# A recurrent attention layer and two gated matrix layers on one core: 64-row transposes on two banks, weight narrowing spread out, and another order of the large units

## The chip, the cores and the metric

The kernel runs on one core of a Trainium2 chip. The metric is the device time of one execution in microseconds (us); lower is better. The kernel before took 459.11 us, the median of three runs (457.83 to 459.53).

The engines are called by the names of the profile: PE is the matrix engine (PEld its weight loads), DVE the vector engine, ACT the scalar engine, POOL the GpSimd engine, and SP the engine that here issues DMAs and empty instructions that only wait. Each engine has its own queue and takes it in order.

## The reference

An mLSTM recurrence (2 batches, 8 heads, 768 steps, head dimension 40) gives 1536 token rows of 320 values, and two gated layers follow, each with three weight matrices of 320x1536, 320x1536 and 1536x320:

```python
def _moe_ref(x, w_gate, w_val, w_out):
    gate = 1.0 / (1.0 + np.exp(-(x @ w_gate)))
    val = x @ w_val
    return (gate * val @ w_out).astype(np.float32)

def _moe2_ref(x, w_a, w_b, w_out):
    a = x @ w_a
    b = x @ w_b
    return (a * b @ w_out).astype(np.float32)
```

The weights of the layers arrive as 64-bit floats and are narrowed on the core. Every product is made of three in the PE's short format: high by high, high by low and low by high, where "low" is what the rounding to "high" left over.

## The kernel before, in words

**Order.** The whole program is one list of task names, the string `PLAN` (lines 67 to 130). The loop at line 890 walks it and calls each task's function (`tasks`, lines 742 to 873), and every engine gets its instructions in that order. A suffix names the engine where a task may run on several: `:V` is DVE, `:G` is POOL, `:A` is ACT. The list also fixes which buffer a task gets: `pick` (line 879) gives it the one whose readers stand earliest in the list. There are two buffers each of `mm1`, `e`, `acc` and `y`, all PSUM banks (line 724).

**Stages.** Up to about 133.6 us the recurrence (24 half steps) is interleaved with 24 small units of the first layer. Then come 60 large units, units 24 to 83. A segment is four large units that share four token tiles of 128 rows and four accumulators: segments 8 to 13 finish the first layer, 14 to 22 make the second.

**A large unit u** takes one chunk (128 of the 1536 hidden columns) and four token tiles (512 rows). On PE it is four tasks, each made of pairs of matmuls on the two 64-row halves of the array (`side_by_side`, line 542): `ma` (8 pairs) and `mb` (7 pairs) make both products into two banks, one `mm1` and one `e`; `mm` and `mn` (6 pairs each) multiply the gated result into the four accumulators. `mb` and `mn` start with a handshake: an empty instruction on SP waits for the last matmuls of `ma` or `mm`, and the first pair of `mb` or `mn` waits for it (lines 544 to 553). It stands in SP's queue between the DMA issues. Between `mb` and `mm` lie `ga_` (ACT, L598: copies one product, with the sigmoid in the first layer), `gm` (DVE, L603: times the other), `gh_` (ACT, L609: the high part) and `gl_` (DVE, L614: the low part). `ma` of unit u+2 needs the banks of unit u, so it waits for `ga_` and `gm` of u.

**A segment's end.** Four tasks `ev<segment>.<tile>` empty the accumulators (L704 adds into `x2tok`; L702 or, on ACT, L700 where it is the first segment of a layer). The first `mm` of the next segment needs the same four banks: its first three pairs need one `acc` and one `y` bank, its last three the other two.

**A weight chunk c** is loaded by `w` (960 KB, SP, L209) and narrowed: `na` (ACT, two instructions, L216 and L217), `nb`, `ns`, `nc` (DVE, L223, L228, L234), `nd` (L240), then split: `s1` (ACT, L250 to L252), `s2` (L256), `s3` (L260, L261). `na` needs the landed data and the one `cva` buffer that `nd` of the chunk before gives back; `w` needs a `wst` buffer that `s2` and `s3` of chunk c-2 give back.

**Between the layers** each of the 12 token tiles is transposed: `yt` (PE, three transposes, L485), `yh` (ACT, L494, the high part) and `yl` (DVE, L498, the low part) write the second layer's input.

Of the kernel before, what the change touches and what calls it, by code (L numbers as in the profile page):

```python
# [96 lines left out]
ma31 ga_30 gm30 mm29 gh_30 gl_30 mb31 s110 mn29 ma32 ga_31 gm31 mm30 gh_31 gl_31 s210:G s310:V mb32 na11 mn30
ma33 ga_32 gm32 mm31 gh_32 gl_32 nb11 ns11 mb33 nc11 nd11:V mn31 w12 ma34 ga_33 ev9.5 ev9.7 ev9.4 ev9.6 gm33
mm32 gh_33 gl_33 mb34 s111 mn32 ma35 ga_34 gm34 mm33 gh_34 gl_34 s211:G s311:V mb35 na12 mn33 ma36 ga_35 gm35
mm34 gh_35 gl_35 nb12 ns12 mb36 nc12 nd12:V mn34 w13 ma37 ga_36 gm36 mm35 gh_36 gl_36 mb37 s112 mn35 ma38  # L100
ga_37 ev10.11 ev10.9 ev10.8 ev10.10 gm37 mm36 gh_37 gl_37 s212:G s312:V mb38 na13 mn36 ma39 ga_38 gm38 mm37
gh_38 gl_38 nb13 ns13 mb39 nc13 nd13:V mn37 w14 ma40 ga_39 gm39 mm38 gh_39 gl_39 mb40 s113 mn38 ma41 ga_40
gm40 mm39 gh_40 gl_40 s213:G s313:V mb41 na14 mn39 ma42 ga_41 ev11.0 ev11.1 ev11.2 ev11.3 gm41 mm40 gh_41
gl_41 nb14 ns14 mb42 nc14 nd14:V mn40 w15 ma43 ga_42 gm42 mm41 gh_42 gl_42 mb43 s114 mn41 ma44 ga_43 gm43 yt0
mm42 yh0 yl0 gh_43 gl_43 s214:G s314:V mb44 na15 mn42 ma45 ga_44 gm44 yt1 mm43 yh1 yl1 gh_44 gl_44 nb15 ns15
mb45 nc15 nd15:V mn43 w16 ma46 ga_45 ev12.4 ev12.6 ev12.5 ev12.7 gm45 yt2 mm44 yh2 yl2 gh_45 gl_45 mb46 s115
mn44 ma47 ga_46 gm46 yt3 mm45 yh3 yl3 gh_46 gl_46 s215:G s315:V mb47 na16 mn45 ma48 ga_47 gm47 yt4 mm46 yh4
yl4 gh_47 gl_47 nb16 ns16 mb48 nc16 nd16:V mn46 w17 ma49 ga_48 gm48 yt6 mm47 yh6 yl6 gh_48 gl_48 mb49 s116
mn47 ma50 ga_49 ev13.10 ev13.8 ev13.11 ev13.9 gm49 yt5 mm48 yh5 yl5 gh_49 gl_49 s216:G s316:V mb50 na17 mn48
ma51 ga_50 gm50 yt7 mm49 yh7 yl7 gh_50 gl_50 nb17 ns17 mb51 nc17 nd17:V mn49 w18 ma52 ga_51 gm51 yt10 mm50  # L110
yh10 yl10 gh_51 gl_51 mb52 s117 mn50 ma53 ga_52 gm52 yt8 mm51 yh8 yl8 gh_52 gl_52 s217:G s317:V mb53 na18 mn51
ma54 ga_53 ev14.2:A ev14.1:V ev14.3:A ev14.0:V gm53 yt11 mm52 yh11 yl11 gh_53 gl_53 nb18 ns18 mb54 nc18 nd18:V
mn52 w19 ma55 ga_54 gm54 yt9 mm53 yh9 yl9 gh_54 gl_54 mb55 s118 mn53 ma56 ga_55 gm55 mm54 gh_55 gl_55 s218:G
s318:V mb56 na19 mn54 ma57 ga_56 gm56 mm55 gh_56 gl_56 nb19 ns19 mb57 nc19 nd19:V mn55 w20 ma58 ga_57 ev15.5:V
ev15.4:V ev15.7:A ev15.6:V gm57 mm56 gh_57 gl_57 mb58 s119 mn56 ma59 ga_58 gm58 mm57 gh_58 gl_58 s219:G s319:V
mb59 na20 mn57 ma60 ga_59 gm59 mm58 gh_59 gl_59 nb20 ns20 mb60 nc20 nd20:V mn58 w21 ma61 ga_60 gm60 mm59 gh_60
gl_60 mb61 s120 mn59 ma62 ga_61 ev16.11:A ev16.8:V ev16.10:V ev16.9:V gm61 mm60 gh_61 gl_61 s220:G s320:V mb62
na21 mn60 ma63 ga_62 gm62 mm61 gh_62 gl_62 nb21 ns21 mb63 nc21 nd21:V mn61 w22 ma64 ga_63 gm63 mm62 gh_63
gl_63 mb64 s121 mn62 ma65 ga_64 gm64 mm63 gh_64 gl_64 s221:G s321:V mb65 na22 mn63 ma66 ga_65 ev17.0 ev17.3
ev17.1 ev17.2 gm65 mm64 gh_65 gl_65 nb22 ns22 mb66 nc22 nd22:V mn64 w23 ma67 ga_66 gm66 mm65 gh_66 gl_66 mb67  # L120
s122 mn65 ma68 ga_67 gm67 mm66 gh_67 gl_67 s222:G s322:V mb68 na23 mn66 ma69 ga_68 gm68 mm67 gh_68 gl_68 nb23
ns23 mb69 nc23 nd23:V mn67 ma70 ga_69 ev18.7 ev18.4 ev18.5 ev18.6 gm69 mm68 gh_69 gl_69 mb70 s123 mn68 ma71
ga_70 gm70 mm69 gh_70 gl_70 s223:G s323:V mb71 mn69 ma72 ga_71 gm71 mm70 gh_71 gl_71 mb72 mn70 ma73 ga_72 gm72
mm71 gh_72 gl_72 mb73 mn71 ma74 ga_73 ev19.10 ev19.11 ev19.8 ev19.9 gm73 mm72 gh_73 gl_73 mb74 mn72 ma75 ga_74
gm74 mm73 gh_74 gl_74 mb75 mn73 ma76 ga_75 gm75 mm74 gh_75 gl_75 mb76 mn74 ma77 ga_76 gm76 mm75 gh_76 gl_76
mb77 mn75 ma78 ga_77 ev20.2 ev20.3 ev20.0 ev20.1 gm77 mm76 gh_77 gl_77 mb78 mn76 ma79 ga_78 gm78 mm77 gh_78
# [886 lines left out]
```

## Time and profile before

| | |
|---|---|
| median of three runs | 459.11 us (457.83 to 459.53) |
| the profiled execution | 459.29 us, its span 457.5 us |
| PE busy | 435.3 us, 95% of the span |
| DVE, ACT, POOL busy | 300.7, 258.0, 107.7 us |
| mean granted PE clock | 0.993 of full |
| large units | from 133.6 us to 451.4 us |

Busy times are sums over the span. A busy PE is not a PE at its peak, since matmuls overlap and their ends are modelled: what a unit costs is read from the distance between starts. A time in a row counts from the start of the span. The device time is 1.8 us above the span.

### The profile page before, as it was taken

The page shows a single profiled execution, that of the slowest core. Times are in us where ns is not written, and L with a number is a line of the kernel's source. Part 1 is how long each engine was busy: PE and PEld are TensorE (multiplying, and loading weights), DVE is VectorE, ACT ScalarE, POOL GpSimd, SP SyncE. Part 2 cuts the span into 40 slices and gives each one's busy share as a digit, 9 for nine tenths or more (in the row PEclk, how much of TensorE's full clock was granted, in tenths as well). Part 3 has the DMA queues.
Part 4 walks back from the last instruction along what each step waited for, and adds up shares of the span by engine and source line. Part 5 has one row for each costly group of instructions (what it writes and reads, how often), then busy time and mean ns, then how long its engine had stood idle before and what let it go on. Part 6 is the DMA issues. An engine that isn't in the chain of part 4 may idle for free.

```text
span 457.5 us, 12013 instructions
## 1 busy us (share of the span) xinstructions
PE 435.3 (95%) x5085; PEld 401.8 (88%) x5090; DVE 300.7 (66%) x512; ACT 258.0 (56%) x455; POOL 107.7 (24%) x108
## 2 busy tenths in 40 slices
...
GB/s 261 240 263 282 153 111 146 264 29 118 87 0 87 28 61 87 87 14 75 87 87 38 51 88 20 69 89 87 1 87 87 87 2 1 0 1 1 59 30 87
DMA packets 10469, 39.54 MB, mean 86 GB/s; under 512 B 1840, under 2 KB 3760, under 8 KB 10416
## 3 DMA queue, kind: packets, MB, share of 16 engines
...
q8 instruction: 40, 0.66, 0.6%
q10 hardware_dynamic: 288, 0.33, 0.2%
...
## 4 chain that ended last, share of the span: by engine, by line
PE 76%; ACT 8%; DVE 8%; DMA 3%; issue 2%; POOL 1%; SPq 1%; DVEq 0%; ACTq 0%; POOLq 0%
PE acc L549 19%; PE pb L549 17%; PE pa L549 17%; PE pa L526 9%; PE o L443 2%; PE sp L414 2%; DMA wst<-in_w_dram 2%; DVE cva L234 2%; DMA og<-in_ogate_dram 1%; PE acc L533 1%; ACT gh L609 1%; PE acc L534 1%; PE acc L535 1%; PE st L433 1%; DVE wst L240 1%
## 5 line engine op out<-in xcount | busy, mean ns | idle before, releaser
L549 PE MATMUL pb<-xb,W 64*128 64x512 f32 x900 | 214.8, 378 | 2.8 <-SPq L545 2.7
L549 PE MATMUL pa<-xb,W 64*128 64x512 f32 x900 | 214.8, 378 | 0.0
L549 PEld LDWEIGHTS pb<-xb,W 64*128 64x128 f32 x900 | 162.4, 187 | 5.8 <-SPq L545 3.5
L549 PEld LDWEIGHTS pa<-xb,W 64*128 64x128 f32 x900 | 162.4, 187 | 2.9 <-issue 0.2
L549 PE MATMUL acc<-W,gh 64*128 64x320 f32 x960 | 114.5, 301 | 6.3 <-DVE x2tok L704 3.6
L549 PEld LDWEIGHTS acc<-W,gh 64*128 64x128 f32 x960 | 102.1, 186 | 12.3 <-issue 5.9
L609 ACT ACTIVATE gh<-g 128x512 fp32r<-128x512 f32 (+1 forms) x84 | 47.6, 567 | 84.2 <-DVE g L603 76.7
L549 PE MATMUL acc<-W,gl 64*128 64x320 f32 x480 | 90.5, 296 | 0.0
L603 DVE TENSOR_TENSOR g<-g,pb 128x512 f32<-128x512 f32 x60 | 41.1, 685 | 65.7 <-ACT g L598 65.7
L256 POOL TENSOR_TENSOR W<-wst,W 128x832 fp32r<-128x832 f32 x17 | 34.4, 2025 | 174.6 <-ACT W L250 148.8
L598 ACT ACTIVATE g<-pa 128x512 f32<-128x512 f32 x60 | 35.7, 595 | 67.2 <-PE pa L549 66.8
L614 DVE TENSOR_TENSOR gl<-g,gh 128x512 fp32r<-128x512 f32 (+1 forms) x67 | 45.7, 682 | 37.5 <-ACT gh L609 37.0
L549 PEld LDWEIGHTS acc<-W,gl 64*128 64x128 f32 x480 | 65.5, 186 | 0.1
L526 PE MATMUL pa<-xb,W 128*128 128x256 f32 x384 | 48.4, 277 | 0.0
L526 PEld LDWEIGHTS pa<-xb,W 128*128 128x128 f32 x384 | 46.0, 192 | 0.7
L216 ACT ACTIVATE cva<-wst 128x960 f32<-128x960 f32 x24 | 31.1, 1296 | 2.2 <-DMA wst<-in_w_dram 1.4
L234 DVE SCALAR_TENSOR_TENSOR cva<-wst,cva 128x960 int32<-128x960 int32 x24 | 31.4, 1309 | 0.6
L704 DVE SCALAR_TENSOR_TENSOR x2tok<-acc,x2tok 128x320 f32<-128x320 f32 x52 | 22.2, 487 | 14.0 <-PE acc L549 13.9
L217 ACT ACTIVATE wst<-wst 128x960 int32<-128x960 uint32 x24 | 30.3, 1263 | 0.0
L240 DVE CUSTOM_DVE_ANT_0 wst<-wst,cva 128x1920 uint16<-128x1920 uint16 x21 | 28.1, 1337 | 2.2
L250 ACT ACTIVATE W<-wst 128x832 fp32r<-128x832 f32 x24 | 27.3, 1139 | 0.1
L614 POOL TENSOR_TENSOR gl<-g,gh 128x256 fp32r<-128x256 f32 x17 | 15.2, 895 | 32.5 <-ACT gh L609 13.3
...
## 6 DMA issues: line engine op xcount, KB each, us to landing
...
rhsE<-V SPq DMA_DIRECT2D x24, 2.0 KB
```

The source lines that it names most:

```text
L216: nc.scalar.activation(cva[0], hi.bitcast(F32), AF.Abs)
L217: nc.scalar.activation(lo, lo.bitcast(U32), AF.Copy, scale=2.0**-29)
L234: nc.vector.scalar_tensor_tensor(ai, hi, -0x40000000, ai, op0=ALU.bitwise_and, op1=ALU.bitwise_or)
L240: e.tensor_tensor(lo, cva[0].bitcast(I32), lo, op=ALU.add)
L250: nc.scalar.activation(w[:, 0:NH], g[:, 0:NH], AF.Copy)
L256: e.tensor_tensor(w[:, NH : 2 * NH], g[:, 0:NH], w[:, 0:NH].bitcast(F32), op=ALU.subtract)
L526: nc.tensor.matmul(dst, w[:, w0 : w0 + P], x[:, h, cb].rearrange("p a b -> p b a"), start=(i == 0), stop=(i == 7))
L549: last = [nc.tensor.matmul(o, w, x, start=st, stop=sp) for o, w, x, st, sp in pair]
L598: nc.scalar.activation(t, pa, AF.Copy if l else AF.Sigmoid)
L603: nc.vector.tensor_tensor(t, t, pb, op=ALU.mult)
L609: nc.scalar.activation(gh, g, AF.Copy)
L614: eng.tensor_tensor(gl, g, gh.bitcast(F32), op=ALU.subtract)
```

## The change

Three things are changed, and all else is left as it was.

The transposes between the layers read the 64 lower and the 64 upper rows of a token tile apart: six transposes of 64 rows by 128 columns in place of three of 128 by 128, the lower half into a bank of `mm1`, the upper half into a bank of `e`. `yh` and `yl` become two instructions each, one for each bank, and `yt` holds a bank of both kinds until `yl` has read them.

The narrowing tasks of chunks 9 to 23 no longer stand close together in the list, and each of `nd`, `s2` and `s3` is on DVE or POOL chunk by chunk. Of chunks 8 to 23 `nd` was on DVE 16 times and is on DVE 7 and POOL 9 times; `s2` was on POOL 16 times and is on POOL 10 and DVE 6 times; `s3` was on DVE 16 times and is on POOL 12 and DVE 4 times.

The order of the list from unit 24 on is another one. The core of the diff, with the stretches of the new order that are spoken of below:

```diff
-nb8 ns8 s37:G mb24 nc8 nd8:V ma25 ga_24 gm24 mm22 mm23 gh_24 gl_24 s27:G w9 mb25 s18 ma26 ga_25 gm25 gh_25
-gl_25 s28:G s38:V ev7.11:V ev7.10:A mm24 mb26 na9 mn24 ma27 ga_26 gm26 mm25 gh_26 gl_26 nb9 ns9 k111:V mb27
...
-gl_32 nb11 ns11 mb33 nc11 nd11:V mn31 w12 ma34 ga_33 ev9.5 ev9.7 ev9.4 ev9.6 gm33 mm32
...
+nb8 ns8 s37:G mb24 nc8 ma25 ga_24 gm24 mm22 mm23 gh_24 gl_24 nd8:V s27:G mb25 s18 w9 ma26 ga_25 gm25 gh_25
+gl_25 s28:G s38:G ev7.11:V ev7.10:A mm24 mb26 na9 mn24 ma27 ga_26 mm25 w10 gm26 mb27 nb9 ns9 ga_27 gh_26 nc9
...
+mn35 w13 gh_37 mb38 gl_36 ev10.8 gl_37 ev10.9 ev10.10 ga_38 ev10.11 gm38 mm36
...
+gl_39 nc13 nd13:V gm40 na14 ga_41 gm41 mm39 s113 gh_40 ma42 mn39 ma43
...
+mb45 mm43 yt1 gh_44 nb15 ga_45 yh1 gl_44 gm45 ns15 yl1 s214:G s314:G
+mn43 ev12.5 ma46 yt2 nc15 gh_45 yh2 ev12.7 ev12.4 yl2 ev12.6 mm44 nd15:G mb46 ma47 ga_46
...
+mb49 nc16 mm47 gh_48 ga_49 nd16:G yt6 gm49 gl_48 mn47 yh6 ma50 w17 yl6
+ev13.10 yt5 ev13.9 na17 ev13.11 nb17 ev13.8 yh5 mm48 mb50 ns17 yl5 mn48
...
+mn59 ev16.10:A ns21 ga_62 ev16.9:V gm62 ev16.11:A gh_61 ma63 ev16.8:A mm60
...
+mm66 mb69 nd22:V ga_68 gm68 mn66 mm67 w23 ma70 na23 ga_69 gh_68 nb23
+gl_68 gm69 mn67 ev18.6 ev18.5 ev18.4 gh_69 ev18.7 mb70 ga_70 ma71 gl_69 ns23 gm70 mm68
...
     def ph_T2(s):
-        Tps[NSTEP + s] = transp(ps_tile("mm1", f"t2_{s}"), x2tok[:, s])
+
+        t2[s] = [ps_tile(b, f"t2{b}_{s}")[:, : 3 * P // 2] for b in ("mm1", "e")]
+        for c in range(3):
+            for rows, t in zip((LOW, UPP), t2[s]):
+                nc.tensor.matmul(
+                    t[:, c * P // 2 : (c + 1) * P // 2], x2tok[rows, s, c * P : (c + 1) * P],
+                    ident[rows, rows].rearrange("p (b a) -> p a b", a=2), start=True, stop=True, is_transpose=True,
+                )
+
+    t2 = {}
+
+    def ph_x2(s, lo):
+        d = xblock(NB + s // NT)
+        for i, t in enumerate(t2[s]):
+            b0 = (s % NT) * (P // 2) + i * P // 4
+            hi, l = (d[:, k, :, :, b0 : b0 + P // 4] for k in (0, 1))
+            t = t.rearrange("p (c a b) -> p c a b", c=3, a=2)
+            if lo:
+                nc.vector.tensor_tensor(l, t, hi.bitcast(F32), op=ALU.subtract)
+            else:
+                nc.scalar.activation(hi, t, AF.Copy)
...
-                task(f"yt{s}", "P", lambda s=s: ph_T2(s), [f"ev{k}.{s}"], [("mm1", [f"yl{s}"])])
-                task(f"yh{s}", "A", lambda s=s: ph_xh(s + NSTEP), [f"yt{s}", f"mb{last_l1[s // NT]}"])
-                task(f"yl{s}", "V", lambda s=s: ph_xl(s + NSTEP), [f"yh{s}"])
+                task(f"yt{s}", "P", lambda s=s: ph_T2(s), [f"ev{k}.{s}"], [("mm1", [f"yl{s}"]), ("e", [f"yl{s}"])])
+                task(f"yh{s}", "A", lambda s=s: ph_x2(s, False), [f"yt{s}", f"mb{last_l1[s // NT]}"])
+                task(f"yl{s}", "V", lambda s=s: ph_x2(s, True), [f"yh{s}"])
```

## Rows read from the trace of the kernel before

**Rows 1.** The page, engines: busy us (share of the span), instructions.
```profile
PE 435.3 (95%) x5085; PEld 401.8 (88%) x5090; DVE 300.7 (66%) x512; ACT 258.0 (56%) x455; POOL 107.7 (24%) x108
```

**Rows 2.** Chain that ended last, 196 to 208 us: start, us, what.
```profile
198.05 0.81 PE acc L549 x12
...
200.37 0.81 PE acc L549 x12
...
202.91 0.81 PE acc L549 x12
```

**Rows 3.** The chain again, 254 to 273 us, where tiles are transposed.
```profile
260.55 1.01 PE acc L549 x12
...
266.09 1.01 PE acc L549 x12
```

**Rows 4.** Timeline of PE: one transpose between the layers, and what follows it.
```profile
304.34 0.55 PE L485 MATMUL t<-cs,x2tok 128*128 128x128 f32 x3
304.82 0.54 PE L549 MATMUL acc<-W,gh 64*128 64x320 f32 x4
```

**Rows 5.** Timeline of PE: a transpose among the small units.
```profile
120.25 0.49 PE L485 MATMUL tp<-cs,xt 128*128 128x128 f32 x3
120.50 0.38 PE L533 MATMUL acc<-W,gh 128*128 128x320 f32 x1
```

**Rows 6.** Waits: who waited for whom: us in total, times, longest.
```profile
PE acc L549 <- DVE x2tok L704: 3.6, 3, 1.5
...
PE acc L549 <- DVE x2tok L702: 2.6, 2, 2.2
```

**Rows 7.** Timeline of DVE at the end of a segment.
```profile
190.50 1.18 DVE L240 CUSTOM_DVE_ANT_0 wst<-wst,cva 128x1920 uint16<-128x1920 uint16 x1
191.58 1.69 DVE L704 SCALAR_TENSOR_TENSOR x2tok<-acc,x2tok 128x320 f32<-128x320 f32 x4
```

**Rows 8.** The chain at the start of the large units, 141 to 152 us.
```profile
141.97 1.99 POOL W L256
...
143.98 0.33 SPq L209
...
144.42 3.16 PE pb L549 x7
```

**Rows 9.** Windows there: length, busy us (count) of PE, PEld, DVE, ACT, POOL, clock, DMA.
```profile
141.70:143.80 2.10, 0.00 (x0) 0.00 (x0) 1.34 (x2) 1.38 (x3) 2.02 (x2) 1.00 0.00 0
143.90:147.20 3.30, 2.78 (x14) 2.23 (x16) 0.60 (x1) 0.51 (x2) 2.44 (x2) 0.50 0.64 214
```

**Rows 10.** DMA, 143 to 153 us in 40 slices of 0.25 us: GB/s.
```profile
GB/s 0 0 0 0 0 0 0 184 61 215 154 246 399 430 461 338 399 399 461 184 0 0 0 0 0 0 0 0 0 0 0 0 0 0 0 0 0 0 0 0
```

**Rows 11.** Groups by line and shape: busy us, mean ns of one, idle before and releasers.
```profile
L614 DVE TENSOR_TENSOR gl<-g,gh 128x512 fp32r<-128x512 f32 x60 | 42.3, 705 | 37.4 <-ACT gh L609 37.0
L603 DVE TENSOR_TENSOR g<-g,pb 128x512 f32<-128x512 f32 x60 | 41.1, 685 | 65.7 <-ACT g L598 65.7
L609 ACT ACTIVATE gh<-g 128x512 fp32r<-128x512 f32 x60 | 37.8, 630 | 77.6 <-DVE g L603 76.7 <-PE acc L549 0.8
L598 ACT ACTIVATE g<-pa 128x512 f32<-128x512 f32 x60 | 35.7, 595 | 67.2 <-PE pa L549 66.8
...
L234 DVE SCALAR_TENSOR_TENSOR cva<-wst,cva 128x960 int32<-128x960 int32 x24 | 31.4, 1309 | 0.6
L216 ACT ACTIVATE cva<-wst 128x960 f32<-128x960 f32 x24 | 31.1, 1296 | 2.2 <-DMA wst<-in_w_dram 1.4 <-POOL wst L240 0.7
...
L223 DVE TENSOR_SCALAR cva<-cva 128x960 f32<-128x960 f32 x24 | 15.9, 663 | 0.8 <-ACT cva L216 0.8
...
L240 POOL TENSOR_TENSOR wst<-cva,wst 128x960 int32<-128x960 int32 x3 | 7.1, 2377 | 4.8 <-ACT Dt L376 4.8
...
L494 ACT ACTIVATE xb<-t 128x384 fp32r<-128x384 f32 x12 | 5.9, 492 | 20.8 <-PE t L485 20.8
```

**Rows 12.** Timeline of DVE while POOL runs the L256 of Rows 8.
```profile
143.08 1.42 DVE L614 TENSOR_TENSOR gl<-g,gh 128x512 fp32r<-128x512 f32 x1 [0.76 <-ACT gh L609]
```

More of the change, by code (lines that the diff above doesn't have):

```diff
@@ L92 @@
 mm20 gh_21 ga_22 gp22 gl_21:G gm22 nd7:G ga_23 na8 gh_22 gp23 k011:G gl_22:G mm21 s17 gm23 ma24 gh_23 gl_23:G
-nb8 ns8 s37:G mb24 nc8 nd8:V ma25 ga_24 gm24 mm22 mm23 gh_24 gl_24 s27:G w9 mb25 s18 ma26 ga_25 gm25 gh_25
-gl_25 s28:G s38:V ev7.11:V ev7.10:A mm24 mb26 na9 mn24 ma27 ga_26 gm26 mm25 gh_26 gl_26 nb9 ns9 k111:V mb27
-nc9 nd9:V mn25 w10 ma28 ga_27 gm27 mm26 gh_27 gl_27 mb28 s19 mn26 ma29 ga_28 gm28 mm27 gh_28 gl_28 s29:G s39:V
-mb29 na10 mn27 ma30 ga_29 ev8.1 ev8.0 ev8.3 ev8.2 gm29 mm28 gh_29 gl_29 nb10 ns10 mb30 nc10 nd10:V mn28 w11
@@ L97 @@
[L97 to L126, printed above, removed]
@@ L127 @@
-gl_78 mb79 mn77 out1 out3 ma80 ga_79 gm79 mm78 gh_79 gl_79 mb80 mn78 ma81 ga_80 gm80 mm79 gh_80 gl_80 mb81
-mn79 ma82 ga_81 ev21.6 ev21.7 ev21.4 ev21.5 gm81 mm80 gh_81 gl_81 mb82 mn80 out7 ma83 ga_82 gm82 mm81 gh_82
-gl_82 mb83 mn81 out5 ga_83 gm83 mm82 gh_83 gl_83 mn82 mm83 mn83 ev22.8 ev22.9 out9 ev22.10 ev22.11 out11
+nb8 ns8 s37:G mb24 nc8 ma25 ga_24 gm24 mm22 mm23 gh_24 gl_24 nd8:V s27:G mb25 s18 w9 ma26 ga_25 gm25 gh_25
+gl_25 s28:G s38:G ev7.11:V ev7.10:A mm24 mb26 na9 mn24 ma27 ga_26 mm25 w10 gm26 mb27 nb9 ns9 ga_27 gh_26 nc9
@@ new lines @@
+ma28 mn25 nd9:G mb28 gm27 na10 gl_26 mm26 ma29 ga_28 gh_27 mn26 mb29 gm28 nb10 gl_27 ga_29 gm29 ma30 mm27 mb30
+mn27 gh_28 s19 gl_28 ns10 ga_30 gh_29 ev8.2 ma31 ev8.1 ev8.3 s29:G ev8.0 gm30 gl_29 mm28 nc10 mb31 nd10:V mn28
+ma32 s39:G ga_31 mm29 s110 gh_30 w11 gm31 mb32 ma33 mn29 gl_30 na11 ga_32 mm30 gh_31 nb11 mb33 mn30 ns11 gm32
+gl_31 s310:G ga_33 gh_32 mm31 s210:G w12 gm33 ma34 gl_32 mn31 nc11 ev9.6 gh_33 ev9.4 ma35 ev9.5 ev9.7 nd11:G
+mm32 mb34 mb35 gl_33 ga_34 mn32 gm34 s111 ma36 mm33 gh_34 ga_35 gm35 mb36 mn33 ma37 gl_34 na12 nb12 gh_35
@@ new lines @@
+ga_36 s311:G gm36 s211:G mm34 mb37 ns12 gl_35 ma38 ga_37 mn34 mm35 gm37 nc12 nd12:G gh_36 ma39 mn35 w13 gh_37
+mb38 gl_36 ev10.8 gl_37 ev10.9 ev10.10 ga_38 ev10.11 gm38 mm36 mb39 na13 s112 ga_39 mn36 mm37 ma40 mn37 mb40
+gm39 s212:V gh_38 ma41 s312:V nb13 gl_38 w14 mm38 mb41 mn38 gh_39 ns13 ga_40 gl_39 nc13 nd13:V gm40 na14 ga_41
+gm41 mm39 s113 gh_40 ma42 mn39 ma43 gh_41 mb42 ev11.2 ev11.1 nb14 ns14 gl_40 ev11.3 ev11.0 gl_41 nc14 mm40
+ga_42 mb43 mn40 gm42 s313:G ga_43 gh_42 gm43 s213:V ma44 nd14:V mm41 gl_42 mb44 ga_44 s114 mn41 gm44 mm42 yt0
@@ new lines @@
+w15 yh0 gh_43 na15 yl0 gl_43 ma45 mn42 mb45 mm43 yt1 gh_44 nb15 ga_45 yh1 gl_44 gm45 ns15 yl1 s214:G s314:G
+mn43 ev12.5 ma46 yt2 nc15 gh_45 yh2 ev12.7 ev12.4 yl2 ev12.6 mm44 nd15:G mb46 ma47 ga_46 gm46 gl_45 yt3 s115
+w16 mn44 yh3 mb47 s215:V yl3 gh_46 ma48 mm45 gl_46 ga_47 gm47 yt4 mb48 mn45 na16 s315:G yh4 gh_47 yl4 nb16
+mm46 ma49 mn46 ga_48 gm48 ns16 gl_47 mb49 nc16 mm47 gh_48 ga_49 nd16:G yt6 gm49 gl_48 mn47 yh6 ma50 w17 yl6
+ev13.10 yt5 ev13.9 na17 ev13.11 nb17 ev13.8 yh5 mm48 mb50 ns17 yl5 mn48 s116 ga_50 ma51 k111:V gh_49 gm50
@@ new lines @@
+gl_49 yt7 mm49 mb51 s216:V nc17 yh7 yl7 mn49 ga_51 gh_50 gm51 ma52 yt10 gl_50 yh10 s316:V mm50 mb52 yl10
+nd17:V gh_51 ga_52 ma53 mn50 w18 s117 gl_51 gm52 mm51 yt8 mb53 yh8 mn51 yl8 ma54 ga_53 gh_52 gm53 ev14.2:A
+s217:G na18 gl_52 ev14.0:V yt11 yh11 ev14.3:V ev14.1:V yl11 mm52 mb54 gh_53 ga_54 mn52 gl_53 gm54 ma55 gh_54
+yt9 mm53 yh9 mb55 nb18 gl_54 ns18 yl9 mn53 mm54 ma56 mn54 s317:G nc18 ga_55 gm55 nd18:G gh_55 mb56 gl_55 ga_56
+s118 s318:V w19 mm55 ma57 na19 mn55 mb57 gm56 ma58 ev15.4:V s218:V ga_57 ev15.5:V gm57 ma59 ev15.7:A nb19
@@ new lines @@
+gh_56 gl_56 ns19 ev15.6:V mb58 gh_57 ga_58 gl_57 w20 nc19 mm56 nd19:V mb59 gm58 mn56 ma60 ga_59 mm57 gh_58
+na20 s119 gl_58 gm59 mb60 mn57 mm58 s319:G ga_60 gh_59 nb20 s219:V gm60 gl_59 ma61 mn58 ns20 nc20 mb61 ma62
+nd20:G w21 mm59 gh_60 ga_61 na21 gl_60 gm61 mb62 nb21 mn59 ev16.10:A ns21 ga_62 ev16.9:V gm62 ev16.11:A gh_61
+ma63 ev16.8:A mm60 mb63 gl_61 mn60 gh_62 ga_63 nc21 gl_62 ma64 mm61 s120 mb64 mn61 gm63 ga_64 gh_63 mm62 gl_63
+s320:G s220:G ma65 mn62 nd21:G gm64 mb65 mm63 gh_64 ma66 w22 ga_65 s121 gl_64 na22 mn63 gm65 ev17.0 nb22 ma67
```

11 lines of the change are left out of this document (added).

## The prediction, made before the changed kernel ran

> **What bounds the kernel now.** The page comes first: PE is busy 95% of the span [rows 1], so an edit pays only if it shortens PE's own work or one of the few waits in it. The chain of waits then gives the price of a unit. The starts of its groups of 12 accumulator matmuls lie 2.32 and 2.54 us apart [rows 2]: a unit costs 4.86 us, of which `mm` and `mn` take 0.81 each, the seven pairs of `mb` 1.51 and the eight of `ma` 1.73. Where tiles are transposed, two starts lie 5.54 us apart [rows 3]: a transpose costs 0.68, twelve of them 8.2. The list of waits gives the rest: PE waits 3.6 us in three places for the additions that empty the accumulators, and in two places 2.6 for the plain copies that do, of which 2.2 belong to the start of the large units [rows 6]. The timeline of DVE shows why: the four additions, 0.42 each, stand in its queue behind the end of a narrowing [rows 7].
>
> **Part 1, transposes.** Three transposes of 128 rows between the 64-row pairs cost 0.68 [rows 3]; the next matmuls start 0.48 after them [rows 4]. Among the small units, where all is 128 rows, they start 0.25 after [rows 5]. So most of the price is the change of shape, which the new form avoids. I take 0.25 for six 64-row transposes, side by side in pairs: 0.43 saved, 12 times, is **-5.2**. The bounds are no gain at all and 0.6 saved each (-7). The second ACT and DVE instructions of each tile add about 0.2 us to a task of 0.49 [rows 11]; they have cover except at segment ends, where I count them.
>
> The trace of the pairs shows 24 weight loads of 128 columns in the 1.62 us of `mm` and `mn`, 0.07 each [rows 2]. The Trainium skill, "TensorE: Matmul & The Clock Gate", section LDWEIGHTS, says that a load costs its columns over 1.2 GHz, whatever the rows: 0.107 us for 128 columns, so six loads in a row would be 0.64, an estimate by that page, and the part would give -0.5. The row is below that price, which the loads of the two halves running side by side would explain.
>
> **Part 2, the old waits.** With narrowing no longer in front of the additions, the waits for them go: 3.6 and 0.4 [rows 6], and up to 1 us more since the next group otherwise overlaps the one before. **-4.5** (-4 to -5).
>
> **Part 3, the new order.** The mean way from `mb` to `mm` of a unit grows from 7.4 to about 10 us of PE work, counted through the list with the prices above. That covers much, but eleven places are left where a queue is late. I walked each queue by hand with the durations of [rows 2, 7, 11].
>
> *The load of chunk 17.* `w17` stands in SP's queue behind the handshake for `mn47`, so it is issued when `mm47` ends. A load takes about 4.1 us from issue to the last byte [rows 8, 10], and the row of SP shows the same order in force: a load that waited for POOL held up the handshake behind it [rows 8]. Behind the load wait the first instruction of `na17` (1.30), `nb17` (0.66) and, behind that on DVE, `ev13.8` (0.42) [rows 7, 11]; with handoffs 6.6. PE meanwhile has `mn47`, `ma50`, a transpose and half of `mm48`: 3.2. **+3.4** (+2.5 to +4).
>
> *The load of chunk 23*, issued when `mm66` ends: 4.1, `na23` 2.6, `ga_69` 0.6, `gh_68` 0.63, `gl_68` 0.7, `gm69` 0.69 [rows 11], 9.4 in all, before `ma71` has a free bank. PE has `mb69`, `mn66`, `mm67`, `ma70`, `mn67`, `mb70`: 7.2. **+2.4** (+1.5 to +3).
>
> *The start of segment 13.* After `gm45`, which frees the bank for `ma46`, DVE has `ns15`, `yl1`, an addition, `nc15`, two additions, `yl2`, an addition: 0.66+0.65+0.42+1.31+0.84+0.65+0.42 = 5.0; PE needs the last 2.4 after the start of `ma46`. **+2.6**; the least is 1.3, by the chain `yt2`, `yh2`, `yl2`, `ev12.6` alone; 3.5 if `na15` on ACT also holds `gm45` back.
>
> *Smaller ones:* `mm36`, with `gl_37` between the additions, +0.6; `ma43`, with `na14` before `ga_41` on ACT, +0.6; `mm60`, with three of four copies on ACT between `ga_62` and `gh_61`, +0.6; `mm40`, `mm52`, `mm72`, `mm80` together +1.1 (each between 0 and its own 0.2 to 0.9).
>
> *The clock.* PE idled for 2.1 us and more at 141.7, and the granted clock was then 0.50 for the 3.3 us in which it worked again [rows 9]. The wait at `mm48` is longer, so I count one such fall; at half the rate those 3.3 us do 1.65 less work: **+1.5** (0 to 1.7).
>
> *The start of the large units.* `w9` moves behind `mb25`, which then no longer waits for POOL to end at 143.96 [rows 8]. But `nd8` now stands behind `gl_24` on DVE, which ends at 144.50 [rows 12]; with its 1.18 [rows 7] it ends at 145.7, the three instructions of `s18` wait for it on ACT, and `ga_25` stands behind them. So of the idle time little is won for `mm24`, the next work on PE that waits: I take 0.9. PE idles some 5 us before it and then starts at the low clock, which costs the 1.5 of above. **+0.6** (-0.9 to +1).
>
> Chunks are ready well before use everywhere: `s2` of chunk 23, the nearest, ends some 5 us of PE work before `ma75`. So where narrowing moves to POOL it costs nothing by itself (2.38 on POOL for `nd` [rows 11], hidden by those units).
>
> **The sum.** -5.2 -4.5 +3.4 +2.4 +2.6 +2.9 +1.5 +0.6 = +3.7. The profiled execution took 459.29, 0.2 above the median: 459.29 + 3.7 gives **463.0 us**.
>
> **Rivals.** *The order has more cover than my walk* (faster): if PE's own delays let DVE and ACT catch up, and the two loads are issued early enough that `na17` and `na23` find their data, the waits of part 3 shrink to the small 2.9 and no clock falls: 459.3 -5.2 -4.5 +2.9 -0.9 = 451.6. It decides at the place of `w17` and `w23` in SP's queue: if they are issued 3.4 and 2.4 us before the ends of `mm47` and `mm66`, no wait is left. For it speaks that all waits are worked out on mean durations; against it, that SP's order is seen in [rows 8].
>
> *In between:* the two load waits stand, the DVE waits vanish: 451.6 +3.4 +2.4 = 457.4, no difference.
>
> *The transposes gain nothing*, so that the edit doesn't do what it says: 463.0 +5.2 = 468.2. Against it are the 0.25 among equal shapes [rows 5].
>
> *POOL holds up DVE.* A `gl` that ran beside POOL took 1.42 in place of 0.705 [rows 11, 12]. With nine more `nd` and twelve more `s3` on POOL, one such delay in each of the six waits where DVE is late gives 6 x 0.7 = 4.2: 467.2. The Trainium skill, "SBUF — State Buffer", section "Who interferes with whom", says that a DVE instruction with two SBUF inputs and a POOL instruction that reads SBUF block each other fully; `gl` is one, and the row agrees.
>
> **How the numbers follow.** Forecast (459.5 to 465.5) 0.47; more cover 0.22; in between 0.17; POOL 0.08; transposes 0.06. The range takes in most of the faster case and the POOL case: 451.5 to 467.5. A measurement tells half a per cent, 2.3 us. Faster (below 456.8): 0.22 and a little of the in between, 0.25. Same: most of the in between and the low end of the forecast, 0.23. Slower: 0.52.
>
> **What would show it.** In the new trace: the starts around a transpose about 0.25 farther apart than without one; no wait of PE for L704 before `mm32` and `mm68`; a wait of about 3 us for the copy of tile 8 at `mm48` with the load of chunk 17 issued right before; a wait of about 2.5 us at `ma71`; the clock at 0.5 after one of them, and around 150 us. If the two load waits are missing, the forecast is wrong by up to 7 us with the clock.

## The result and the profile after

The changed kernel takes 465.24 us (median of 11 runs, 460.09 to 467.02), the kernel before 459.17 in the runs beside it (455.63 to 461.93): a ratio of 1.0103 with a 95% interval of 1.0062 to 1.0144. It is slower, as forecast (463.0), but the median lies 2.2 us above the forecast. Its runs lie in two groups, five from 460.1 to 462.8 and six from 465.2 to 467.0, and the median is the lowest of the upper group. The profiled execution of the changed kernel took 461.29, its span 459.5.

One line each of the page of the changed kernel, first the engines (busy us, share of the span, instructions), then the granted PE clock in 40 slices:

```profile
PE 436.3 (95%) x5121; PEld 399.9 (87%) x5126; DVE 291.0 (63%) x496; ACT 257.8 (56%) x468; POOL 132.9 (29%) x135
...
PEclk9999999999998899999999997999999999999998
```

Against [rows 1], DVE has lost 9.7 us and POOL has gained 25.2: the narrowing did move. PE is as busy as before, and that hides two opposite things, shorter work and a lower clock. The clock row shows where the clock was lower: low digits in slices 13 and 14, the start of the large units, and in slice 25, which is `mm48`.

In the code of the changed kernel every line of the functions stands one lower than before (L704 is now L705). Its list of waits of PE (us in total, times, longest):

```profile
PE acc L550 <- DVE x2tok L705: 5.6, 5, 3.4
PE acc L550 <- DVE x2tok L703: 5.4, 1, 5.4
PE pb L550 <- DVE g L604: 1.7, 2, 1.4
...
PE pa L550 <- ACT g L599: 1.0, 1, 1.0
...
PE acc L550 <- ACT x2tok L701: 0.3, 1, 0.3
```

The waits of [rows 6] at `mm32` and `mm68` are gone. In their place stand the 3.4 at `mm48`, 1.0 + 1.4 at `ma71` (the rows of L599 and L604), and three of 0.33, 0.86 and 0.52 at the start of segment 13. The 5.4 is the wait before `mm24`.

The chain of waits at `mm48` (start us, us, what; the pieces between are left out):

```profile
269.69 0.02 SPq L546
...
269.83 4.54 DMA wst<-in_w_dram
...
274.46 1.07 ACT cva L217
...
275.55 0.66 DVE cva L224
276.21 0.41 DVE x2tok L705
...
276.67 1.17 PE acc L550 x6
```

It is read downwards: SP ends the handshake, issues the load of chunk 17 right behind it, 4.54 us later the data are there, ACT and DVE narrow, and only then does DVE come to the addition that `mm48` waits for. In the last row six accumulator matmuls take 1.17 us, where twelve take 0.81 in the rows of a transpose below: PE starts again at the low clock.

The same chain at `ma71`, with the load of chunk 23:

```profile
373.52 0.02 SPq L546
...
373.72 4.84 DMA wst<-in_w_dram
...
379.93 1.24 ACT wst L218
381.17 0.49 ACT g L599
381.66 0.53 ACT gh L610
...
382.21 0.69 DVE gl L615
382.90 0.61 DVE g L604
```

The chain around a transpose between the layers:

```profile
286.86 0.81 PE acc L550 x12
...
289.40 0.05 PE t2mm L724
289.45 0.00 PE t2e L724
289.46 0.07 PE t2mm L724
289.52 0.00 PE t2e L724
289.53 0.06 PE t2mm L724
...
289.59 0.87 PE acc L550 x12
```

From the first transpose to the next matmul it is 0.19 us here, where it was 0.48 in [rows 4]; the 12 matmuls behind take 0.87, where they took 1.01 in [rows 3]. The starts of two `mm` in the same view:

```profile
284.48 0.87 PE acc L550 x12
...
299.79 0.52 PE acc L550 x6
```

Between them lie three units with three transposes, 15.31 us; three units without a transpose took 3 x 4.86 = 14.58 before [rows 2]. So a transpose costs 0.24 where nothing waits, as the prediction took it (0.25), against 0.68.

Windows over the stretches at the low clock, first of the changed kernel at the start of the large units and behind `mm48` (length, busy us and count of PE, PEld, DVE, ACT, POOL, granted clock, DMA share, GB/s):

```profile
146.10:152.90 6.80, 5.38 (x32) 4.98 (x34) 1.09 (x2) 2.72 (x5) 1.12 (x2) 0.50 0.31 103
275.80:282.60 6.80, 5.93 (x34) 5.25 (x36) 3.37 (x8) 3.72 (x8) 0.60 (x1) 0.50 0.01 2
```

Before, there was one such stretch in the large units, 3.4 us long, with 2.8 of PE work in it [rows 9]. Both stretches of the changed kernel begin within an idle time of PE, of 5.4 and of 3.4 us, and at a clock of 0.50 (1.2 of 2.4 GHz) PE does half the work. So the stretches cost half of PE's busy time in them: 2.7 and 3.0, against 1.4 before.

**How the runs are compared below.** A difference of a few us is blurred by the clock, since how long a stretch lasts differs from run to run. So each kernel has more measures beside its median: the mean of the runs compared, and in the same runs the mean time at half clock, worked out of the granted clock of each run as (1 - clock) x 2 x its time. Half of that time is the most that the clock can cost. The median is that of all runs, while the means and intervals leave out the runs that lie over 1.5% above the fastest of their kernel: one each of the changed kernel, e2, e4, e5 and e6, and three of the kernel before. The last two columns are those of the *stage*, from the first matmul of `ma24` to the end of the last accumulator matmul, in the profiled execution; "at full clock" takes off half of PE's busy time in that stage's stretches at 0.50. It leaves out the part up to `ma24`, whose length differs from profile to profile (`ma24` starts between 131.0 and 135.2 us in the twelve profiles).

| kernel | median us | mean us | ratio to before, 95% | us at half clock | stage | at full clock |
|---|---|---|---|---|---|---|
| before | 459.17 | 459.3 | | 9.3 | 317.8 | 316.4 |
| changed | 465.24 | 463.7 | 1.0062 to 1.0144 | 16.4 | 322.8 | 317.1 |
| e1, both loads early | 453.68 | 454.5 | 0.9826 to 0.9970 | 10.2 | 314.0 | 311.3 |
| e9, load 17 early | 458.76 | 458.6 | 0.9953 to 1.0014 | 12.6 | 318.3 | 314.0 |
| e10, load 23 early | 459.92 | 460.1 | 0.9970 to 1.0040 | 16.3 | 315.9 | 314.3 |
| e2, old transposes | 465.77 | 464.7 | 1.0042 to 1.0247 | 12.1 | 323.8 | 320.7 |
| e5, e1 + old transposes | 458.03 | 458.5 | 0.9956 to 1.0030 | 12.0 | 317.4 | 314.7 |
| e3, transposes alone | 463.54 | 463.5 | 1.0052 to 1.0126 | 9.3 | 323.4 | 318.9 |
| e4, `nd8` early | 463.39 | 462.4 | 1.0029 to 1.0119 | 15.9 | 318.7 | 315.2 |
| e6, e1 + `nd` on DVE | 454.91 | 455.1 | 0.9854 to 0.9950 | 8.5 | 313.3 | 311.9 |
| e7, e1 + segment 13 | 452.96 | 453.9 | 0.9871 to 0.9940 | 10.3 | 313.0 | 311.3 |
| e8, all of these | 447.69 | 448.3 | 0.9712 to 0.9843 | 5.8 | 307.4 | 307.4 |

The kernel before took 458.8 to 459.5 in the medians beside the experiments; its mean and its time at half clock are of those 64 runs. The table already says the main thing of the result: at full clock the stages of the two kernels are 0.8 us apart (0.77 before rounding). The rest is the clock: 4.2 of the stage's 5.0 us, and in the runs up to (16.4 - 9.3) / 2 = 3.5 of the 4.4 between the means.

Windows over the whole stage show what the 0.8 is made of (length, PE busy and count, clock, DMA share, GB/s), for the kernel before, the changed kernel, e1 and e5:

```profile
133.61:451.40 317.79, 308.27 (x3289) 0.99 0.16 52
130.96:453.74 322.78, 308.34 (x3325) 0.98 0.15 51
132.19:446.14 313.95, 304.71 (x3325) 0.99 0.16 53
135.24:452.67 317.43, 309.02 (x3289) 0.99 0.16 52
```

With half of the busy time at 0.50 taken off, PE works 306.9 us before and 302.7 in the changed kernel: 4.2 less work, and 4.9 more idle time (14.4 against 9.5).

### The profile page after: what moved, and what is told of

The parts are those of the page before. It is cut to its first block, busy times and chain, and to the rows that moved or that the text cites. A ratio compares the mean times of both kernels' runs of the same rounds, so it can differ in the third digit from the quotient of the medians.

```text
span 459.5 us, 12087 instructions
## 1 busy us (share of the span) xinstructions
PE 436.3 (95%) x5121; PEld 399.9 (87%) x5126; DVE 291.0 (63%) x496; ACT 257.8 (56%) x468; POOL 132.9 (29%) x135
## 4 chain that ended last, share of the span: by engine, by line
PE 78%; DMA 8%; DVE 5%; ACT 4%; issue 2%; SPq 2%; POOL 0%; DVEq 0%; ACTq 0%
PE acc L550 20%; PE pb L550 18%; PE pa L550 18%; PE pa L527 9%; DMA wst<-in_w_dram 4%; PE o L444 2%; PE sp L415 2%; DMA Y<-in_kv_dram 2%; DMA og<-in_ogate_dram 1%; PE acc L534 1%; DVE x2tok L705 1%; PE st L434 1%; PE acc L536 1%; PE acc L535 1%; DVE gl L615 1%
## 5 line engine op out<-in xcount | busy, mean ns | idle before, releaser
L550 PEld LDWEIGHTS pb<-xb,W 64*128 64x128 f32 x900 | 164.3, 189 | 8.5 <-DVE g L604 2.5
L550 PE MATMUL acc<-W,gh 64*128 64x320 f32 x960 | 112.6, 305 | 11.6 <-DVE x2tok L705 5.6
L550 PEld LDWEIGHTS acc<-W,gh 64*128 64x128 f32 x960 | 98.1, 190 | 16.5 <-DVE x2tok L705 7.1
L550 PE MATMUL acc<-W,gl 64*128 64x320 f32 x480 | 88.1, 300 | 0.0
L599 ACT ACTIVATE g<-pa 128x512 f32<-128x512 f32 x60 | 35.7, 595 | 91.4 <-PE pa L550 86.4
L604 DVE TENSOR_TENSOR g<-g,pb 128x512 f32<-128x512 f32 x60 | 41.2, 686 | 68.2 <-ACT g L599 67.9
L615 DVE TENSOR_TENSOR gl<-g,gh 128x512 fp32r<-128x512 f32 (+1 forms) x67 | 51.2, 764 | 39.5 <-ACT gh L610 38.4
L550 PEld LDWEIGHTS acc<-W,gl 64*128 64x128 f32 x480 | 63.3, 190 | 0.1
L241 POOL TENSOR_TENSOR wst<-cva,wst 128x960 int32<-128x960 int32 x12 | 28.1, 2346 | 56.6 <-DVE cva L235 30.6
L257 POOL TENSOR_TENSOR W<-wst,W 128x832 fp32r<-128x832 f32 x11 | 22.7, 2065 | 64.9 <-ACT W L251 58.4
L705 DVE SCALAR_TENSOR_TENSOR x2tok<-acc,x2tok 128x320 f32<-128x320 f32 x52 | 22.9, 484 | 13.3 <-PE acc L550 13.2
L261 POOL TENSOR_TENSOR W<-wst,W 64x128 fp32r<-64x128 f32 x19 | 13.3, 698 | 55.0 <-ACT W L252 30.4
```

The source lines that it names most:

```text
L241: e.tensor_tensor(lo, cva[0].bitcast(I32), lo, op=ALU.add)
L550: last = [nc.tensor.matmul(o, w, x, start=st, stop=sp) for o, w, x, st, sp in pair]
L599: nc.scalar.activation(t, pa, AF.Copy if l else AF.Sigmoid)
L604: nc.vector.tensor_tensor(t, t, pb, op=ALU.mult)
L615: eng.tensor_tensor(gl, g, gh.bitcast(F32), op=ALU.subtract)
L705: nc.vector.scalar_tensor_tensor(dst[:, 0:DM], acc, half, dst[:, 0:DM], op0=ALU.mult, op1=ALU.add)
```

## The experiments

### Both loads issued earlier (e1_loads_early)

In the list of tasks of the changed kernel the two loads move ahead of the handshakes that they stood behind (the list is cut at each `...`):

```diff
-... gl_48 mn47 yh6 ma50 w17 yl6 ev13.10 ...
+... gl_48 mn47 yh6 ma50 yl6 ev13.10 ...
-... mb48 mn45 na16 s315:G yh4 gh_47 ...
+... mb48 mn45 na16 s315:G w17 yh4 gh_47 ...
-... mn66 mm67 w23 ma70 na23 ...
+... mn66 mm67 ma70 na23 ...
-... ma68 gl_66 s321:V ma69 mn65 ...
+... ma68 gl_66 s321:V w23 ma69 mn65 ...
```

> The changed kernel with two tasks of the list moved: the load of chunk 17 from behind ma50 to behind s3 of chunk 15, the load of chunk 23 from behind mn66 to behind s3 of chunk 21, so that both are issued as soon as their buffer is free and no longer wait for a handshake of PE. Theory of the loads (the place of a load in SP's queue sets the waits at mm48 and ma71): the wait of PE at mm48, 3.4 us in the trace after, falls under 0.6, the waits at ma71, 1.0 and 1.4, fall under 0.5 together, and the half clock from 275.8 us on, which the first of them brings, does not come; together 5 to 9 us less than the changed kernel, 457 to 460 in the scale of its median of 465.2. Rival (DVE's own queue is late at mm48 and ACT's at ma71, the loads only seem to be last): at most 1.5 us less, the waits stay above 2 and 1.5 us.

Measured: 453.68, a ratio of 0.9898 to before; 11.6 under the changed kernel. PE's waits for the additions and copies:

```profile
PE acc L550 <- DVE x2tok L703: 5.4, 1, 5.4
PE acc L550 <- DVE x2tok L705: 2.9, 5, 0.9
```

The 3.4 at `mm48` has become 0.7, the wait at `ma71` is gone, and the stretch at half clock behind `mm48` with them. At full clock the stage is 5.8 shorter, where the waits alone give 2.7 + 2.4 = 5.1. So the places of the two issues are the cause of both waits. That the time fell by more than the waits was not settled by this run.

### Each load alone (e9_load17_alone, e10_load23_alone)

The same edit, one load at a time.

> The changed kernel with the load of chunk 17 alone issued earlier (ahead of the handshake for mn47, as in e1_loads_early); the load of chunk 23 stays behind its handshake. Theory, each load pays by its own wait, and the one at mm48 also by the clock: the wait at mm48 goes from 3.4 to about 0.7 us (2.7), and the half clock of 6.8 us behind it goes, which costs 3.4: 6.1 under the changed kernel, about 459 us. Rival, the 11.6 us of e1_loads_early come from both loads alike, since the wait at ma71 is only the visible part: then this run gains no more than about 4 and stands near 461.

> The changed kernel with the load of chunk 23 alone issued earlier; the load of chunk 17 stays behind its handshake. Theory: only the 2.4 us of wait at ma71 go and the half clock behind mm48 stays: about 463 us. Rival, both loads alike: some 6 us under the changed kernel, about 459. The two savings of this run and e9_load17_alone should add up to that of e1_loads_early (11.6) if the loads are all that it changed; by the theory they add up to 8.5, and 3 us stay open.

Measured: 458.76 and 459.92, savings of 6.5 and 5.3, 11.8 together against 11.6 in e1. So the savings add up. The first is near the 6.1 of its theory. The second is double what the theory said and near its rival; by the means the savings are 5.1 and 3.6, and the second lies between the two. At full clock the stages are 3.2 and 2.8 shorter, close to the waits of 2.7 and 2.4, so what is over in the second is not more waiting. The profile of e10 shows the window behind `mm48`, after a wait there of 3.6 us:

```profile
279.40:286.20 6.80, 6.79 (x78) 6.21 (x80) 5.33 (x10) 3.69 (x9) 0.60 (x1) 1.00 0.01 2
```

and that of e9 the window behind `ma71`, after waits of 0.9 and 1.4:

```profile
380.30:383.70 3.40, 3.40 (x24) 2.99 (x22) 2.63 (x6) 1.86 (x4) 1.98 (x1) 0.50 0.00 0
```

In the changed kernel's own profile it is the other way round: the low clock comes behind `mm48` and not behind `ma71`. So neither wait draws the low clock always, and either can; the theory, which gave the whole clock to `mm48`, was wrong in that. The runs are in line with it: the time at half clock falls from 16.4 to 12.6 with load 17 early, not at all with load 23 alone (16.3), and to 10.2 with both. But the four runs of e1 have from 7 to 15.5 us of it, so the last step is not sure. Half of that and the waits together, 2.7 + 1.9, 2.4 + 0.1 and 5.1 + 3.1, are 4.6, 2.5 and 8.2; the means of the runs fell by 5.1, 3.6 and 9.2. So waits and clock explain most of what the two loads cost. The last 0.5 to 1.1 us is within what the intervals leave open.

### The old transposes in the new order (e2_old_transposes, e5_loads_old_transposes)

The changed kernel, and e1, with `yt`, `yh` and `yl` as they were, one bank and three transposes of 128 rows:

```diff
-        t2[s] = [ps_tile(b, f"t2{b}_{s}")[:, : 3 * P // 2] for b in ("mm1", "e")]
...
+        Tps[NSTEP + s] = transp(ps_tile("mm1", f"t2_{s}"), x2tok[:, s])
```

> The changed kernel with the order and the engines of the change, but with the transposes between the layers as before: three of 128 by 128 into one bank, one copy and one subtraction for a tile. Theory of the shape (most of a transpose's 0.68 us is the change from 64-row to 128-row matmuls and back): each of the 12 transposes costs some 0.4 us more on PE again, 3 to 5 us in all, less where a wait for DVE or ACT hides it: 468 to 470. Rival (the way a transpose is cut makes no difference, the distance of starts was the order's): within 1 us of the changed kernel.

> The changed kernel with the two loads early, and with the transposes of the kernel before (three of 128 by 128, one bank). Beside the run with the loads early it prices the 64-row form where no fall of the clock hides or doubles it. Theory of the shape: each transpose 0.3 to 0.43 us dearer on PE, so 3.5 to 5.2 us more than with the loads early (453.7): 457 to 459. Rival (the form of the transposes is worth nothing even here): 453 to 455.

Measured: 465.77 against 465.24 for the changed kernel, no difference that can be told from four runs (462.67 to 472.03); and 458.03 against 453.68 for e1, 4.3 more. So the times of e2 spoke for the rival that the transposes are worth nothing, and those of e5 against it. The stages at full clock agree with each other: +3.5 and +3.4. e2's stage has half as much time at half clock as the changed kernel's (6.8 against 13.7 us), which hides the difference in the time. In each of these two, 0.9 to 1.0 is not PE's own work but a wait of the last accumulator matmuls for a handshake that stood behind an issue of the output on SP. That leaves 2.6 and 2.4 us that the new shape gains at the end. It saves more on PE: in the slower form PE comes later to the waits behind the transposes, and these are shorter by 1.9 in e2 (3.4 to 2.8, 0.86 to 0.46, and 0.52 and 0.33 gone) and by 1.6 in e5. PE's busy time at full clock says the same without the waits: 307.0 in e2 against 302.7 in the changed kernel, 306.3 in e5 against 302.1 in e1. So PE's own saving is 4.2 to 4.3 us, and 1.6 to 1.9 of it only lengthens waits for DVE.

### The transposes alone (e3_transposes_alone)

The kernel before with the new transposes and nothing else; of the edit the line that asks for the second bank:

```diff
...
-                task(f"yt{s}", "P", lambda s=s: ph_T2(s), [f"ev{k}.{s}"], [("mm1", [f"yl{s}"])])
+                task(f"yt{s}", "P", lambda s=s: ph_T2(s), [f"ev{k}.{s}"], [("mm1", [f"yl{s}"]), ("e", [f"yl{s}"])])
...
```

> The kernel before with the 64-row transposes alone: its order of tasks and its engines are left as they were. Theory of the shape: a start after a transpose lies about 0.25 us farther from the last one in place of 0.68, 12 times: 5.2 us less, 454 against 459.2, and the rest of the change is then worth +9 to +11. Rival (the transposes are no cheaper, the new order alone makes the difference): within 1.5 us of the kernel before. A second rival (a bank of both kinds held by a transpose makes the next unit wait): slower than before by 1 to 3 us, with new waits of ma for yl.

Measured: 463.54, a ratio of 1.0089: slower, by some 4 us. The list of waits of this kernel (its lines are those of before):

```profile
PE t2e L723 <- DVE g L603: 8.3, 6, 3.2
```

and its timeline at the first of them:

```profile
252.03 1.17 DVE L240 CUSTOM_DVE_ANT_0 wst<-wst,cva 128x1920 uint16<-128x1920 uint16 x1
252.05 0.22 PE L723 MATMUL t2mm<-cs,x2tok 64*128 64x64 f32 x1
253.11 1.69 DVE L704 SCALAR_TENSOR_TENSOR x2tok<-acc,x2tok 128x320 f32<-128x320 f32 x4
...
254.70 0.69 DVE L603 TENSOR_TENSOR g<-g,pb 128x512 f32<-128x512 f32 x1
...
255.44 0.36 PE L723 MATMUL t2e<-cs,x2tok 64*128 64x64 f32 x1 [3.17 <-DVE g L603]
```

The new form needs a bank of `e` as well, and that is held until `gm` has read it. In the old order DVE comes to that `gm` only behind the end of a narrowing (L240) and the four additions (L704), and PE stands at the transposes meanwhile. Six such waits, 8.3 us, are more than the transposes save (PE's busy time at full clock is 302.9, 4.0 less than before), even though the waits of [rows 6] shrink to 2.9 and 1.2 here. So the edit pays only together with an order in which `gm` is early. The second rival was nearest to this, but it is the transpose that waits, and not the next unit. The prediction priced the part as if it stood by itself and did not see this; the sum did not suffer, since the new order has the cover.

### The start of the large units (e4_nd8_early)

The narrowing step `nd8` of the changed kernel stands ahead of `ma25` again, as before:

```diff
-... mm23 gh_24 gl_24 nd8:V s27:G mb25 ...
+... mm23 gh_24 gl_24 s27:G mb25 ...
-... nc8 ma25 ga_24 gm24 mm22 ...
+... nc8 nd8:V ma25 ga_24 gm24 mm22 ...
```

> The changed kernel with one task moved: nd of chunk 8 stands again before ma25, as in the kernel before, and not behind gl_24. Theory of the queue (s18 waits for nd8 on ACT, ga_25 waits behind s18, so mm24 comes late): ga_25 starts about 2.3 us earlier after gl_24 and the idle time of PE before mm24, 5.4 us in the trace after, falls to about 3; the half clock there, 6.8 us long, gets shorter or stays: 2 to 4.5 us less than the changed kernel. Rival (mm24 waits for the emptying of the small units' banks for another reason): no difference, the idle time stays above 5.

Measured: 463.39, 1.9 under the changed kernel, which the intervals do not tell from nothing; the stage at full clock 1.9 shorter. The wait before `mm24`:

```profile
PE acc L550 <- DVE x2tok L703: 3.1, 1, 3.1
```

It was 5.4. So `nd8` behind `gl_24` does hold up `s18`, `ga_25` and the copies, as the walk of the queues said, for 2.3 of the 5.4 us; the gain is just under the 2 to 4.5 that were expected.

### Narrowing on DVE or POOL (e6_nd_on_dve)

e1 with nine `nd` tasks back on DVE:

```diff
-... nd9:G ... nd11:G ...
+... nd9:V ... nd11:V ...
```

> The changed kernel with the two loads early, and with the nine nd tasks that run on POOL put on DVE; the order is left. Theory that POOL's steps cost nothing by themselves: within 1.5 us of the run with the loads early, 452 to 455.5; DVE has 9 times 1.3 us more, a gl beside POOL goes back from over 1.0 us to 0.7. Rival (POOL holds up DVE's subtractions, and this is on the path): 2 to 4 us less, 450 to 452. The other side (DVE's queue is so full that nd on it makes the segments' ends wait): 2 us and more above, over 456.

Measured: 454.91 against 453.68 for e1, no difference that these runs tell (at full clock 0.6 more). The groups of `gl` by shape, first in the changed kernel, where the `nd` run on POOL (e1 has 797 ns):

```profile
L615 DVE TENSOR_TENSOR gl<-g,gh 128x512 fp32r<-128x512 f32 x60 | 47.8, 796 | 39.5 <-ACT gh L610 38.4 <-PE pa L550 0.8
```

and in e6:

```profile
L615 DVE TENSOR_TENSOR gl<-g,gh 128x512 fp32r<-128x512 f32 x60 | 42.9, 715 | 37.9 <-ACT gh L610 36.7 <-PE pa L550 0.8
```

A mean `gl` takes 0.08 us longer when POOL narrows, 4.9 us over 60 of them. So `gl` is slower beside the narrowing on POOL. The Trainium skill, "SBUF — State Buffer", section "Who interferes with whom", says that a DVE instruction with two SBUF inputs contends with a POOL instruction that reads SBUF. The rows agree, at 796 against 715 ns. But DVE is off PE's path nearly everywhere: taking the delay away, at the price of nine more narrowing steps on DVE, is worth nothing. The steps `s2` and `s3` were not moved alone in any run.

### Segment 13 (e7_segment13)

e1 with the additions directly behind the transpose, and `nc15` behind `mm44`:

```diff
-... ma46 yt2 nc15 gh_45 yh2 ev12.7 ev12.4 yl2 ev12.6 mm44 nd15:G ...
+... ma46 yt2 ev12.7 ev12.4 ev12.6 gh_45 yh2 yl2 mm44 nc15 nd15:G ...
```

> The changed kernel with the two loads early, and at the start of segment 13 with the three last additions put directly behind yt2, ahead of yl2, and nc of chunk 15 behind mm44. Theory of DVE's queue there (nc15 and yl2 ahead of the additions make mm44 wait): the waits at mm44, 0.9 and 0.5 us with the loads early, go, that of ma46 (0.2) stays: 1.2 to 1.5 us less, 452.3. Rival (the transposes' own chain holds mm44, whatever stands on DVE): no difference, and the waits stay.

Measured: 452.96 against 453.68, not to be told apart, and the same stage at full clock. The waits at L705 fell from 2.9 to 1.5, but a new one of 0.6, for the low part of a transposed tile, and other small shifts took that back: which wait ends last at this place was only exchanged.

### All together (e8_all_three)

e7 with `nd8` as in e4, and with the tasks that stood between PE and its next accumulators moved:

```diff
-... mm23 gh_24 gl_24 nd8:V s27:G mb25 s18 w9 ma26 ga_25 gm25 gh_25 gl_25 ...
+... mm23 gh_24 ev7.10:A gl_24 ev7.11:V s27:G mb25 w9 ma26 ga_25 gm25 gh_25 s18 gl_25 ...
-... s28:G s38:G ev7.11:V ev7.10:A mm24 ...
+... s28:G s38:G mm24 ...
-... ev10.8 gl_37 ev10.9 ev10.10 ga_38 ...
+... ev10.8 ev10.9 ev10.10 gl_37 ga_38 ...
-... ev16.9:V gm62 ev16.11:A gh_61 ma63 ev16.8:A mm60 ...
+... ev16.9:V ev16.8:V gm62 ev16.11:A gh_61 ma63 mm60 ...
```

> The changed kernel with the two loads early, segment 13 as in the run on it, and the start of the large units mended: nd8 ahead of ma25, the last two of the small units' accumulators emptied behind gh_24 and gl_24 and no longer behind gl_25, s18 behind gh_25; also gl_37 behind the third addition of its segment, and the copy ev16.8 on DVE. Theory (mm24 waits for an emptying that stands behind gl_25 in DVE's queue, and the idle time before it brings the half clock): the idle time of 5.4 us before mm24 falls under 1, the half clock from 147 us on, 6.8 us long, does not come: 8 to 10 us less than with the loads early, 444 to 446, faster than both kernels. Rival (the start waits for the next thing, gl_24 or the load w9, and the clock falls all the same): 450 to 453.

Measured: 447.69 (four runs, 446.38 to 451.5), a ratio of 0.9777 to before: faster than both kernels. That is 1.7 above the upper end of what was expected. The clock row of its page, and its waits for accumulators:

```profile
PEclk9999999999999999999999999999999999999998
```

```profile
PE acc L550 <- DVE x2tok L705: 1.0, 2, 0.7
PE acc L550 <- DVE gl L615: 0.9, 1, 0.9
```

The 5.4 before `mm24` is gone, for `mm24` starts right behind the work before it:

```profile
142.85 0.43 PE L550 MATMUL acc<-W,gh 64*128 64x320 f32 x4
```

The 0.9 among the waits is a later one, at 155.8, for `gl_26`. No wait of PE in the stage is longer than that, and in this profile no stretch at half clock is left but the tail of the kernel. So the change gains 2.2% with these moves in its order, and loses 1% with the order that it came with. What the same moves would gain beside the old spread of the narrowing, no run shows.

## Why the prediction was right, step by step

The measured column comes from the two profiled executions; for the transposes the runs e2, e3 and e5 give 4.0 to 4.3.

| step | predicted us | measured us |
|---|---|---|
| transposes | -5.2 | -4.2 |
| old waits | -4.5 | -3.9 |
| load of chunk 17, at `mm48` | +3.4 | +3.4 |
| load of chunk 23, at `ma71` | +2.4 | +2.4 |
| start of segment 13 | +2.6 | +1.7 |
| smaller waits | +2.9 | +1.1 |
| start of the large units, idle | -0.9 | 0.0 |
| the same, clock | +1.5 | +1.3 |
| clock behind `mm48` | +1.5 | +3.0 |
| sum | +3.7 | +4.8; the stage +5.0 |

**The two loads** came out as walked, and e1, e9 and e10 show that the place of the issue in SP's queue is their cause. For chunk 17 the chain from issue to addition took 6.8 us against 6.6 in the walk, and PE had 3.4 of work against 3.2. These two loads took 4.5 and 4.8 rather than 4.1, and the narrowing behind them a little less. For chunk 23 the 2.4 was met partly by luck: the terms of the walk, 9.4 less PE's 7.2, leave 2.2 and not the 2.4 of the sum, and measured were 10.0 and 7.7. The rival that the order has more cover fell at the point that the prediction named: the loads were not issued early.

**The transposes** were the right mechanism, with the right price where nothing waits (0.24, saved 0.44). But that price holds in half of the places: from the first transpose to the next work it takes 0.15 to 0.19 us in six of the twelve, 0.25 to 0.39 in five, and in one, in segment 13, PE waits. So PE saves 4.2 and not 5.2, and of that 1.6 to 1.9 goes to waits for DVE. The five dearer places are those where the two halves of the array are out of step: the first transpose of the upper half starts 0.10 to 0.13 us after that of the lower half, and in the six cheap ones 0.00. In each half, the last of the three starts some 0.12 after the first at all twelve. One of the five, in the timeline:

```profile
269.40 0.28 PE L724 MATMUL t2mm<-cs,x2tok 64*128 64x64 f32 x2
269.50 0.22 PE L724 MATMUL t2e<-cs,x2tok 64*128 64x64 f32 x1
```

So most of what they take longer is this offset, which the matmuls before them already have; where it comes from stays open. The rival of no gain fell by e5.

By the price of the Trainium skill, "TensorE: Matmul & The Clock Gate", section LDWEIGHTS, six loads in a row take 0.64 us, an estimate by that page. The trace does not agree with that as the price of a transpose, which with its six loads adds 0.24. The loads do not run in a row: they start in pairs, one on each half, at 289.02, 289.24 and 289.30, and the first pair runs beside the matmuls before the transpose:

```profile
289.02 0.14 PEld L724 LDWEIGHTS t2mm<-cs,x2tok 64*128 64x128 f32 x1
289.02 0.38 PE L550 MATMUL pa<-xb,W 64*128 64x512 f32 x1
289.03 0.14 PEld L724 LDWEIGHTS t2e<-cs,x2tok 64*128 64x128 f32 x1
```

And e3 shows what the step left out altogether, the second bank: alone, the edit is a loss.

**Segment 13 and the smaller waits** were too dear by 2.7 together. `mm36`, `mm60` and `mm80` waited 0.48, 0.30 and 0.35; `ma43`, `mm40`, `mm52` and `mm72` not at all. The walk added mean durations from a common start; that ACT and DVE were further ahead than that wherever PE had just been held up is likely, but no run here shows it.

**The start of the large units.** The idle of some 5 us before `mm24` is there (5.38), in part for the reason given (e4). But it replaced waits of 2.7, 2.2 and 0.4 in the kernel before, so it was no gain. The 2.2 is in [rows 6], the others are these:

```profile
PE pb L549 <- SPq L545: 2.7, 1, 2.7
...
PE acc L535 <- POOL gl L614: 0.4, 1, 0.4
```

**The clock** was the step that failed. I added 3.3 us of work at half clock twice, as in [rows 9], at the start and behind `mm48`. But the stretch of [rows 9] is the one at the start of the kernel before, and its 1.4 us are already in the 459.29: another of that length there adds nothing. In the changed kernel's profile both stretches are 6.8 long. So the one behind `mm48` cost 3.0, double its term, and the +1.3 at the start, near the 1.5 of its term, is luck. Over the runs the time at half clock is 7.1 us more than before, which costs up to 3.5 against the 3.0 of the two terms: the mean is near, and the single stretch can't be foretold from its wait.

**The sum.** Four errors made it too low (clock at `mm48` 1.5, transposes 1.0, the idle at the start 0.9, old waits 0.6) and three too high (small waits 1.8, segment 13 0.9, clock at the start 0.2). What is left is 1.1, so the sum is nearer than its terms because their errors cancel, which is luck; the median lies 2.2 above the forecast, the mean 0.7. The profiled execution shows only 2.0 us more than before in place of 5, mostly since its `ma24` starts 2.6 earlier (131.0 against 133.6), which is the part that differs from profile to profile.

**The rival POOL** showed its mechanism and, for `nd`, no price (e6).
